# Low halves of the second weights: from scaled differences on VectorE to plain ones on GpSimd, after scaling the weights in place, by quarters, with a side step in every step of a pair

## The chip, the cores and the metric

The kernel runs on one core of a Trainium2 chip. The metric is device time in microseconds (us); the median of three runs of the kernel before is 1008.27 us, and they lie between 1008.16 and 1008.62.

## The reference

Attention with a window of 128 and a linear position bias is followed by a soft mixture of experts (`_moe_ref`, 32 slots) and by a second mixture whose gate is balanced by eight Sinkhorn rounds. The change is in the second mixture, which takes most of the time:

```python
def _moe2_ref(x, w_gate, w1, w2):          # x 2304x512, w1 8x512x1024, w2 8x1024x512
    logits = x @ w_gate
    P = np.exp(logits - logits.max())
    for _ in range(8):
        P /= P.sum(1, keepdims=True) + 1e-09
        P /= P.sum(0, keepdims=True) + 1e-09
        P *= N / E
    out = np.zeros((N, D))
    for e in range(E):
        h = np.maximum(x @ w1[e], 0.0)
        out += P[:, e:e + 1] * (h @ w2[e])
    return out
```

## The kernel before

**The loop.** The second mixture runs over 8 experts (0 to 7) and, in each, over 9 pairs of token tiles. A pair `m` is `relu(x @ w1) @ w2` for two tiles of 128 tokens and is done by Strassen's scheme with seven products. Each product is `prod`: 12 matmuls of 128x128 by 128x256 in float16, in which either factor is split into a high half and a low half (high by high, high by low, low by high). Products go into the PSUM tiles `x` and `y`, and `add` accumulates them into `acc` on VectorE (DVE) by a `scalar_tensor_tensor`; in expert 0 ScalarE (ACT) copies the four first ones.

**A pair's seven steps.** In step `k_` (0 to 6) of pair `m` the program emits, in this order: half of the hidden matmuls `z` of the next pair (`emit_z`, steps 0 and 1, four matmuls each), the product and an `add` (`step`), one piece of side work (`next(side, None)`), and `left(m + 1, k_)`, which builds the left operands of the next pair from `z`. Every engine works through its own instructions in that order. `left` makes the sums `s3`, `s2`, `s1`, `s4` on VectorE, their high halves on ScalarE (`hi_s`) and their low halves on GpSimd (POOL, `lo_s`), in steps 2, 3, 4 and 6. Strassen's second product comes first in a pair, so the low half of `s2`, made in step 3 of one pair, is read at the start of the next. The other low halves have more time.

**Side work.** `side` is a chain of generators; one `yield` is one slot. During expert `e` it holds, for expert `e + 1`: `prep_w1` (5 slots: matmuls with the raw first weights, a scale, the stacked operand `stk`), a load, `prep_w2a` (below), a load of the second weights of `e + 2` into the buffer just read, and `scale_p`. In expert 0 the gate (6 slots) comes first and then the Sinkhorn rounds, three slots each, one slot of them together with one slot of the chain above (`par`). What is left of `side` at step 2 of an expert's last pair is emitted there at once.

**`prep_w2a`.** It finds the largest absolute weight (8 slots of ScalarE's `Abs`, then 4 more) and a power of two `iv`. From the four blocks `b11`, `b12`, `b21`, `b22` of the raw weights it makes Strassen's seven right operands: four differences on GpSimd (`diff`, two instructions of 512 elements per partition each), and for every operand four quarters `r` of 256 elements: the high half `Copy(scale=iv)` on ScalarE (`conv`, L600) and the low half `raw * iv - high` on VectorE (`low`, L593). The queue `todo` holds each low half back by one quarter. Operands are done one after the other, 28 quarters in 28 slots, with the differences riding along. The weights of expert 0 are prepared ahead of the loop.

Of the kernel before, what the change touches and what calls it, by code (L numbers as in the profile page):

```python
# [11 lines left out]
AF = mybir.ActivationFunctionType  # L12
ALU = mybir.AluOpType
# [11 lines left out]
def tile_kernel(ctx: ExitStack, tc: tile.TileContext, q, k, v, phi, w1, w2, w_gate, m1, m2, rel, out):  # L25
    nc = tc.nc
# [68 lines left out]
    with tc.manual_schedule():  # L95
        with ExitStack() as ab:
# [5 lines left out]
            with ExitStack() as at:  # L102
# [369 lines left out]
                side = []  # L472
# [82 lines left out]
            def largest(dg, ps):  # L555
                nc.tensor.matmul(ps, lhsT=ones, rhs=dg, start=True, stop=True)

            def prep_w2a(e, place):
                wsum[e] = mp.tile([128, 4, 256], F32, tag="t1", name="t1", bufs=1)

                am = mp.tile([128, 1], F32, tag="am2", name="am2")
                amp = mp.tile([128, FC], F32, tag="amp", name="amp")
                for i in range(FC):
                    nc.scalar.activation(out=wsum[e][:, 0:2].rearrange("p a b -> p (a b)"),
                                         in_=wt["m2", e][:, DM * i:DM * (i + 1)], func=AF.Abs, accum_out=amp[:, i:i + 1])
                    yield
                yield
                nc.vector.tensor_reduce(out=am, in_=amp, axis=AX.X, op=ALU.max)
                dg = spread(am)
                yield  # L570
                ps = place()
                largest(dg, ps)
                if e:
                    yield
                ar = mp.tile([128, 1], F32, tag="ar2", name="ar2")
                nc.vector.tensor_reduce(out=ar, in_=ps, axis=AX.X, op=ALU.max)
                pw, iv = pow2(mp, ar, "w2")
                nc.vector.tensor_scalar_mul(inv_w[:, e:e + 1], pw, 1.0 / (WSC * CSC))
                nc.vector.tensor_scalar_mul(iv, iv, WSC)  # L579
                yield  # L580
                hi = wpre.tile([128, 7, 4, 256], F16, tag="w", name="w2h")
                lo = wpre.tile([128, 7, 4, 256], F16, tag="w", name="w2l")
                w2c[e] = (hi, lo)


                raw = wt["m2", e].rearrange("p (c f) -> p c f", c=FC)
                b11, b12 = raw[:, 0:4, 0:256], raw[:, 0:4, 256:512]
                b21, b22 = raw[:, 4:8, 0:256], raw[:, 4:8, 256:512]
                t1 = wsum.pop(e)


                def low(i, src, r):
                    nc.vector.scalar_tensor_tensor(out=lo[:, i, r], in0=src[:, r], scalar=iv, in1=hi[:, i, r],  # L593
                                                   op0=ALU.mult, op1=ALU.subtract)

                todo = []

                def conv(i, src):
                    for r in range(4):
                        nc.scalar.activation(out=hi[:, i, r], in_=src[:, r], func=AF.Copy, scale=iv)  # L600
                        if todo:
                            low(*todo.pop())
                        todo.append((i, src, r))
                        yield

                def diff(dst, x_, y_):
                    for r in range(2):
                        eng = nc.gpsimd if e or r else nc.vector
                        eng.tensor_tensor(out=dst[:, 2 * r:2 * r + 2], in0=x_[:, 2 * r:2 * r + 2],
                                          in1=y_[:, 2 * r:2 * r + 2], op=ALU.subtract)  # L610
                        yield

                def both(x_, y_):
                    for _ in x_:
                        next(y_, None)
                        yield

                yield from diff(t1, b12, b11)
                yield from both(conv(0, b11), diff(b12, b22, b12))
                yield from both(conv(2, b21), diff(b11, b22, t1))  # L620
                yield from conv(3, b12)
                yield from both(conv(1, b11), diff(b21, b21, b11))
                yield from conv(4, t1)
                yield from conv(6, b22)
                yield from conv(5, b21)
                low(*todo.pop())
                yield

            def prep_w1(e, pool=None, tag=None):
# [46 lines left out]
            with ExitStack() as bs:  # L676
# [75 lines left out]
                for i in range(4):  # L752
                    for cp in range(4):
                        dst = selh if cp < 2 else sell
                        nc.vector.tensor_copy(out=dst[32 * i:32 * i + 32, 32 * cp:32 * cp + 32],
                                              in_=idn[32 * i:32 * i + 32, 32 * i:32 * i + 32])
# [65 lines left out]
                for h in range(2):  # L822
                    ps = pb.tile([128, 512], F32, tag="b", name="b")
                    for dc in (2 * h, 2 * h + 1):
# [3 lines left out]
                        out=st[:, 2 * h:2 * h + 2], in_=ps[:, 2 * NS * h:2 * NS * h + 2 * NS].rearrange("p (a b) -> p a b", a=2))  # L828
# [7 lines left out]
            with ExitStack() as ms:  # L836
# [271 lines left out]
                side = None  # L1108
                for m in range(NM):
                    e, n = divmod(m, NP)  # L1110
                    if n == 0:
                        side = []
                        if e + 1 < E:
                            side = [prep_w1(e + 1), loads(e + 2, "m1"), prep_w2a(e + 1, lambda: pmt[:, 256:384]), loads(e + 2, "m2")]
                        if e == 0:
                            side = [gate(), par(chain(sinkhorn(), scale_p(0)), chain(*side))]
                        if e + 1 < E:
                            side.append(scale_p(e + 1))
                        side = chain(*side)
                    for k_ in range(7):  # L1120
                        if m and k_ < 2 and m + 1 < NM:
                            emit_z(m + 1, k_)
                        if m or k_ > 3:
                            step(m, k_)
                        elif k_ == 0:

                            step(m, 0)
                            emit_z(m + 1, 0)
                            step(m, 1)
                            step(m, 2)  # L1130
                        elif k_ == 1:
                            emit_z(m + 1, 1)
                            for kk_, nm in ((KS1, "s1"), (KS4, "s4")):
                                hi_s(0, kk_, nm)
                                lo_s(0, kk_, nm)
                            step(m, 3)
                        if k_ == 0:
                            if m:
                                last(m - 1)
                            left(m, 7)  # L1140
                        if k_ != 3:
                            next(side, None)
                        if k_ in (4, 5) and NP - 1 <= m < 2 * NP - 1:
                            weigh((m + 1) % NP + NP * (k_ - 4))
                        if m + 1 < NM:
                            left(m + 1, k_)
                        if n == NP - 1 and k_ == 2:
                            for _ in side:
                                pass
# [38 lines left out]
```

## Time and profile before

| | |
|---|---|
| median of the runs | 1008.27 us |
| the profiled execution | 1009.35 us |
| its span, first to last instruction | 1007.6 us |
| mean granted TensorE clock | 0.99 |
| busy share: TensorE matmul, VectorE, ScalarE, GpSimd | 95%, 84%, 60%, 45% |

The profiled execution lies 1.08 us above the median, and 1.75 us of its time lie outside its span. Times of rows are counted from the span's start. A busy share is a mean over stages: the second mixture begins at about 211 us, and its stages differ. Matmuls are pipelined (one of these takes 273 ns and the next starts 109 ns later), so TensorE's pace is read from where its instructions start. The granted clock is 1.00 where TensorE has its full 2.4 GHz.

### The profile page before, as it was taken

How to read it: one execution, taken by the hardware profiler on the slowest of the kernel's cores; microseconds unless marked ns; L12 is line 12 of the kernel's file. 1: busy time of each engine (PE TensorE's matmuls, PEld its weight loads, DVE VectorE, ACT ScalarE, POOL GpSimd, SP SyncE). 2: the span in 40 equal slices, each digit the busy share in tenths (PEclk: the TensorE clock that was granted, in tenths of full speed). 3: DMA queues.
4: the chain of work that ended last, by engine and by line, in shares of the span. 5: the costliest groups of instructions: out<-in, count | busy, mean ns of one | idle time of the engine just before them, and what ended most of it. 6: DMA issues, size and time to landing. Idle time of an engine off the chain costs nothing.

```text
span 1007.6 us, 24024 instructions
## 1 busy us (share of the span) xinstructions
PE 958.6 (95%) x9341; PEld 811.4 (81%) x9341; DVE 849.7 (84%) x2128; ACT 608.2 (60%) x1473; POOL 452.6 (45%) x433
## 2 busy tenths in 40 slices
PE   8999999888889999999999999999999999999993
PEld 7887886367678888888888888888888888888883
DVE  6888885758999789979988998799789978987772
ACT  5878784745557677665646664656556655654440
POOL 2321211213445475437544754574366447544440
PEclk9999999999999999999999999999999999999997
DMA  9999998941100310220022002200220200001111
GB/s 175 252 236 199 253 289 300 392 178 34 62 2 1 121 60 1 84 95 2 1 85 94 2 1 88 92 1 11 85 86 1 85 12 2 1 1 39 52 53 48
DMA packets 93927, 90.07 MB, mean 89 GB/s; under 512 B 63094, under 2 KB 67062, under 8 KB 93814
## 3 DMA queue, kind: packets, MB, share of 16 engines
q1 hardware_dynamic: 93814, 88.54, 29.5%
q8 instruction: 73, 1.20, 0.5%
q14 instruction: 40, 0.33, 0.1%
HBM read 81.97 MB, written 4.72 MB: 86 GB/s over the span
## 4 chain that ended last, share of the span: by engine, by line
PE 70%; DVE 20%; ACT 5%; issue 3%; DMA 1%; POOL 0%; DVEq 0%; POOLq 0%; SPq 0%; ACTq 0%
PE x L996 27%; PE y L996 21%; PE z L924 5%; DVE w2l L593 4%; PE xp L276 4%; DVE acc L1010 3%; DVE s L949 3%; PE s L202 3%; DVE ops L937 2%; PE pt L251 2%; PE pt L155 2%; PE m L633 1%; ACT w2h L600 1%; PE b L732 1%; ACT ops L934 1%
## 5 line engine op out<-in xcount | busy, mean ns | idle before, releaser
L996 PEld LDWEIGHTS <-ops 128*128 128x128 f16 x6048 | 593.4, 98 | 85.8 <-issue 13.5
L956 POOL TENSOR_TENSOR ops<-s,ops 128x512 f16<-128x512 f32 x287 | 332.3, 1160 | 377.7 <-ACT ops L953 333.4
L996 PE MATMUL x<-w2h,ops 128*128 128x256 f16 x2304 | 415.5, 273 | 5.7 <-DVE acc L1010 3.1
L953 ACT CAST ops<-s 128x512 f16<-128x512 f32 x288 | 177.6, 617 | 267.0 <-DVE s L949 265.6
L996 PE MATMUL y<-w2h,ops 128*128 128x256 f16 x1728 | 320.3, 274 | 4.5 <-DVE acc L1010 4.2
L996 PE MATMUL x<-w2l,ops 128*128 128x256 f16 x1152 | 314.3, 273 | 0.0
L996 PE MATMUL y<-w2l,ops 128*128 128x256 f16 x864 | 236.0, 274 | 0.0
L1010 DVE SCALAR_TENSOR_TENSOR acc<-x,pe,acc 128x256 f32<-128x256 f32 x252 | 120.2, 477 | 34.0 <-PE x L996 33.8
L937 DVE SCALAR_TENSOR_TENSOR ops<-z,ops 128x512 f16<-128x512 f32 x216 | 146.7, 679 | 0.0
L934 ACT ACTIVATE ops<-z 128x512 f16<-128x512 f32 x216 | 127.8, 592 | 25.7 <-PE z L924 23.2
L593 DVE SCALAR_TENSOR_TENSOR w2l<-w,w2i,w2h 128x256 f16<-128x256 f32 x192 | 124.2, 657 | 0.7 <-ACT w2h L600 0.7
L1010 DVE SCALAR_TENSOR_TENSOR acc<-y,pe,acc 128x256 f32<-128x256 f32 x189 | 90.2, 477 | 31.3 <-PE y L996 30.8
L949 DVE SCALAR_TENSOR_TENSOR s<-z,s 128x512 f32<-128x512 f32 x144 | 97.9, 680 | 3.2 <-ACT ops L934 3.1
L949 DVE SCALAR_TENSOR_TENSOR s<-z,r 128x512 f32<-128x512 f32 x144 | 98.0, 680 | 2.8 <-ACT ops L934 2.6
L924 PE MATMUL z<-ct,stk 128*128 128x256 f16 x576 | 87.7, 276 | 7.4 <-DVE ops L937 6.3
L600 ACT ACTIVATE w2h<-w,w2i 128x256 f16<-128x256 f32 x192 | 93.3, 504 | 1.9 <-DVE w2i L579 1.1
L181 POOL TENSOR_SCALAR qn<-qn 128x128 f32<-128x128 f32 x64 | 34.4, 546 | 101.0 <-DMA qn<-in_q_dram 80.6
L924 PEld LDWEIGHTS <-stk 128*128 128x128 f16 x576 | 53.2, 98 | 24.5 <-DVE ops L937 12.2
L230 ACT ACTIVATE et<-et,mx 128x192 f32<-128x192 f32 (+2 forms) x144 | 61.3, 435 | 1.2 <-DVE mx L221 1.1
L202 PE MATMUL s<-kT,qT 128*128 128x192 f32 (+2 forms) x288 | 50.2, 317 | 0.1
L221 DVE CUSTOM_DVE_ANT_0 et<-s,rel_sb 128x192 f32<-128x192 f32 (+2 forms) x144 | 40.2, 326 | 8.6 <-PE s L202 8.1
L202 PEld LDWEIGHTS s<-kT,qT 128*128 128x128 f32 x288 | 43.9, 191 | 3.4 <-issue 3.4
(189 smaller groups left out, 895.4 us busy)
## 6 DMA issues: line engine op xcount, KB each, us to landing
w<-in_moe_w_dram SPq DMA_DIRECT2D x68, 512.0 KB
w<-in_moe_w_dram SPq DMA_DIRECT2D x14, 2048.0 KB
kn<-in_k_dram SPq DMA_DIRECT2D x36, 128.0 KB
qn<-in_q_dram SPq DMA_DIRECT2D x36, 128.0 KB
v<-in_v_dram SPq DMA_DIRECT2D x18, 256.0 KB
out_dram<-acc SPq DMA_DIRECT2D x17, 256.0 KB
w<-in_moe_w_dram SPq DMA_DIRECT2D x2, 1024.0 KB
stk<-sh SPq DMA_DIRECT2D x56, 16.0 KB
```

Of the source, the lines that this page charges most:

```text
L202: nc.tensor.matmul(ps[gg][:, j, col:192], lhsT=qT[:, g, j, :], rhs=kT[:, g, j, k0:k1], start=True, stop=True)
L230: nc.scalar.activation(out=runs[hh], in_=runs[hh], func=AF.Exp, bias=mx[:, hh:hh + 1], scale=-1.0, accum_out=sm[:, hh:hh + 1])
L593: nc.vector.scalar_tensor_tensor(out=lo[:, i, r], in0=src[:, r], scalar=iv, in1=hi[:, i, r], op0=ALU.mult, op1=ALU.subtract)
L600: nc.scalar.activation(out=hi[:, i, r], in_=src[:, r], func=AF.Copy, scale=iv)
L924: nc.tensor.matmul(ps[:, i], lhsT=stk[e][:, 128 * ft:128 * ft + 128], rhs=ct.rearrange("p (a n) t -> p a n t", a=2)[:, :, n, :], start=Tru ...
L934: nc.scalar.activation(out=ops_[m][:, k_, 0], in_=zb(m, i, j), func=AF.Relu)
L937: nc.vector.scalar_tensor_tensor(out=ops_[m][:, k_, 1], in0=zb(m, i, j), scalar=0.0, in1=ops_[m][:, k_, 0], op0=ALU.max, op1=ALU.subtract)
L949: nc.vector.scalar_tensor_tensor(out=new_sum(m, nm), in0=zb(m, i, j), scalar=0.0, in1=o, op0=ALU.max, op1=op)
L953: nc.scalar.copy(out=ops_[m][:, k_, 0], in_=sm_[m, nm])
L956: eng.tensor_tensor(out=ops_[m][:, k_, 1], in0=sm_[m, nm], in1=ops_[m][:, k_, 0], op=ALU.subtract)
L996: nc.tensor.matmul(out_, lhsT=a_[:, k_, l_, i, :], rhs=r_[:, k_, i, :], start=(first and j == 0), stop=(j == 11), skip_group_check=True)
L1010: nc.vector.scalar_tensor_tensor(out=o, in0=ps, scalar=pe_[e][:, t:t + 1], in1=o, op0=ALU.mult, op1=ALU.add)
```

## The change

For expert 0 nothing changes in `prep_w2a`. For the others ScalarE first multiplies the raw weights by `iv` in place, by quarters, two instructions of 512 elements each. High halves are then plain copies (`nc.scalar.copy`), low halves plain differences on GpSimd (`minus`), and the four differences are also made by quarters, all on GpSimd. The loop over quarters is the outer one: 11 slots a quarter, with one GpSimd instruction of 256 elements in each (the first `part` emits none, a last one follows), 45 slots in all, where the weights' conversion and differences took 31. The loop over pairs gives side work a slot in all seven steps; step 3 had none.

```diff
-                yield from diff(t1, b12, b11)
-                yield from both(conv(0, b11), diff(b12, b22, b12))
...
-                yield from conv(5, b21)
-                low(*todo.pop())
+                if e == 0:
+                    yield from diff(t1, b12, b11)
...
+                    return
...
+                def minus(out_, x_, y_):
+                    nc.gpsimd.tensor_tensor(out=out_, in0=x_, in1=y_, op=ALU.subtract)
+
+                def part(i, src, r):
+                    nc.scalar.copy(out=hi[:, i, r], in_=src[:, r])
+                    if todo:
+                        i_, src_, r_ = todo.pop()
+                        minus(lo[:, i_, r_], src_[:, r_], hi[:, i_, r_])
+                    todo.append((i, src, r))
+
+                for r in range(4):
+                    for x_ in (raw[:, r, :], raw[:, r + 4, :]):
+                        nc.scalar.activation(out=x_, in_=x_, func=AF.Copy, scale=iv)
+                    minus(t1[:, r], b12[:, r], b11[:, r])
+                    yield
+                    part(0, b11, r)
+                    yield
+                    minus(b12[:, r], b22[:, r], b12[:, r])
+                    yield
+                    part(2, b21, r)
+                    yield
+                    minus(b11[:, r], b22[:, r], t1[:, r])
+                    yield
+                    part(3, b12, r)
+                    yield
+                    part(1, b11, r)
+                    yield
+                    minus(b21[:, r], b21[:, r], b11[:, r])
+                    yield
+                    part(4, t1, r)
+                    yield
+                    part(6, b22, r)
+                    yield
+                    part(5, b21, r)
+                    yield
...
-                        if k_ != 3:
-                            next(side, None)
+                        next(side, None)
```

Line numbers behind the changed place rise: `low`'s L593 stays for expert 0 alone, `minus` is L634, and L937, L949, L956, L1010 become L980, L992, L999, L1053.

On VectorE, late in a pair of expert 1, the program had the following. `s_...` rows are the sums of the next pair (the first one `s1`, the last `s4`), `acc` rows the accumulation, and `w2l` rows the low halves of the coming weights:

```order
L949 SCALAR_TENSOR_TENSOR s_6030<-z,r_5953 128x512
L1010 SCALAR_TENSOR_TENSOR acc<-x,pe,acc 128x256
L593 SCALAR_TENSOR_TENSOR w2l<-w,w2i,w2h 128x256
L937 SCALAR_TENSOR_TENSOR ops<-z,ops 128x512
L1010 SCALAR_TENSOR_TENSOR acc<-x,pe,acc 128x256
L593 SCALAR_TENSOR_TENSOR w2l<-w,w2i,w2h 128x256
L949 SCALAR_TENSOR_TENSOR s_6067<-z,s_6010 128x512
L1010 SCALAR_TENSOR_TENSOR acc<-y,pe,acc 128x256
```

Now the same place on VectorE reads:

```order
L992 SCALAR_TENSOR_TENSOR s_6050<-z,r_5973 128x512
L1053 SCALAR_TENSOR_TENSOR acc<-x,pe,acc 128x256
L980 SCALAR_TENSOR_TENSOR ops<-z,ops 128x512
L1053 SCALAR_TENSOR_TENSOR acc<-x,pe,acc 128x256
L992 SCALAR_TENSOR_TENSOR s_6087<-z,s_6031 128x512
L1053 SCALAR_TENSOR_TENSOR acc<-y,pe,acc 128x256
```

The `w2l` rows are gone from it, and nothing stands in their place. On GpSimd the pair of which this is the end had only the four `lo_s` in most pairs of an expert (`ops` rows, of `s3`, `s2`, `s1`, `s4` in this order). Now it has, from behind the `lo_s` of the pair before to its own last one:

```order
L634 TENSOR_TENSOR w2l<-w,w2h 128x256
L634 TENSOR_TENSOR w<-w 128x256
L634 TENSOR_TENSOR w2l<-w,w2h 128x256
L999 TENSOR_TENSOR ops<-s_5994,ops 128x512
L634 TENSOR_TENSOR w2l<-w,w2h 128x256
L999 TENSOR_TENSOR ops<-s_6031,ops 128x512
L634 TENSOR_TENSOR w<-w 128x256
L999 TENSOR_TENSOR ops<-s_6050,ops 128x512
L634 TENSOR_TENSOR w2l<-w,w2h 128x256
L634 TENSOR_TENSOR w2l<-t_5209,w2h 128x256
L999 TENSOR_TENSOR ops<-s_6087,ops 128x512
```

Seven instructions came in: three ahead of `s3`'s low half, one ahead of `s2`'s, one ahead of `s1`'s, two ahead of `s4`'s. The third place is GpSimd at the end of expert 0, where what is left of `side` is emitted at once, between the `lo_s` of `s3` (first row) and of `s2` (last row) of the first pair of expert 1:

```order
L999 TENSOR_TENSOR ops<-s_4938,ops 128x512
L634 TENSOR_TENSOR w2l<-w,w2h 128x256
L634 TENSOR_TENSOR w<-w,t_3922 128x256
L634 TENSOR_TENSOR w2l<-w,w2h 128x256 x2
L634 TENSOR_TENSOR w<-w 128x256
L634 TENSOR_TENSOR w2l<-w,w2h 128x256
L634 TENSOR_TENSOR w2l<-t_3922,w2h 128x256
L634 TENSOR_TENSOR w2l<-w,w2h 128x256 x2
L999 TENSOR_TENSOR ops<-s_4991,ops 128x512
```

Nine instructions stand there where before none stood; at the ends of experts 1 to 6 it is three.

## Rows read from the trace of the kernel before

**Rows 1.** The page's first part: busy time, share of the span, instructions, by engine.

```profile
PE 958.6 (95%) x9341; PEld 811.4 (81%) x9341; DVE 849.7 (84%) x2128; ACT 608.2 (60%) x1473; POOL 452.6 (45%) x433
```

**Rows 2.** TensorE's timeline, first `z` matmul of six pairs: start, length, instruction.

```profile
229.17 0.38 PE L924 MATMUL z<-ct,stk 128*128 128x256 f16 x2
...
331.19 0.38 PE L924 MATMUL z<-ct,stk 128*128 128x256 f16 x2
...
630.43 0.38 PE L924 MATMUL z<-ct,stk 128*128 128x256 f16 x2
...
640.48 0.38 PE L924 MATMUL z<-ct,stk 128*128 128x256 f16 x2
...
660.79 0.38 PE L924 MATMUL z<-ct,stk 128*128 128x256 f16 x2
...
712.74 0.27 PE L924 MATMUL z<-ct,stk 128*128 128x256 f16 x1
```

**Rows 3.** Busy time by stretch, three pairs of expert 4: length, then each engine's.

```profile
core 0: us, PE busy (x) PEld busy (x) DVE busy (x) ACT busy (x) POOL busy (x), PEclk, DMA share, GB/s
...
630.90:640.90 10.00, 10.00 (x94) 8.98 (x92) 7.53 (x15) 8.09 (x21) 4.63 (x4) 1.00 0.45 157
...
651.20:661.20 10.00, 10.00 (x94) 8.96 (x92) 8.77 (x18) 6.39 (x13) 9.05 (x9) 1.00 0.01 2
661.20:672.10 10.90, 10.52 (x95) 8.97 (x94) 10.90 (x21) 6.85 (x14) 7.05 (x6) 1.00 0.01 2
```

**Rows 4.** The page's costliest groups: instruction, count, busy us, mean ns, idle before.

```profile
L956 POOL TENSOR_TENSOR ops<-s,ops 128x512 f16<-128x512 f32 x287 | 332.3, 1160 | 377.7 <-ACT ops L953 333.4
...
L593 DVE SCALAR_TENSOR_TENSOR w2l<-w,w2i,w2h 128x256 f16<-128x256 f32 x192 | 124.2, 657 | 0.7 <-ACT w2h L600 0.7
...
L600 ACT ACTIVATE w2h<-w,w2i 128x256 f16<-128x256 f32 x192 | 93.3, 504 | 1.9 <-DVE w2i L579 1.1
```

**Rows 5.** VectorE's timeline, four instructions.

```profile
239.89 0.18 DVE L881 TENSOR_SCALAR rs<-rs 128x18 f32<-128x18 f32 x1
...
252.12 1.08 DVE L881 TENSOR_SCALAR rs<-rs 128x18 f32<-128x18 f32 x1
...
662.58 1.26 DVE L593 SCALAR_TENSOR_TENSOR w2l<-w,w2i,w2h 128x256 f16<-128x256 f32 x1
...
666.18 0.47 DVE L593 SCALAR_TENSOR_TENSOR w2l<-w,w2i,w2h 128x256 f16<-128x256 f32 x1
```

**Rows 6.** GpSimd's timeline, one pair of expert 4; in brackets the idle time before.

```profile
634.95 1.16 POOL L956 TENSOR_TENSOR ops<-s,ops 128x512 f16<-128x512 f32 x1 [2.65 <-ACT ops L953]
637.25 1.16 POOL L956 TENSOR_TENSOR ops<-s,ops 128x512 f16<-128x512 f32 x1 [1.15 <-ACT ops L953]
638.56 1.16 POOL L956 TENSOR_TENSOR ops<-s,ops 128x512 f16<-128x512 f32 x1 [0.15 <-ACT ops L953]
641.18 1.16 POOL L956 TENSOR_TENSOR ops<-s,ops 128x512 f16<-128x512 f32 x1 [1.46 <-ACT ops L953]
```

**Rows 7.** GpSimd's groups by form, whole program: two of them.

```profile
L181 POOL TENSOR_SCALAR qn<-qn 128x128 f32<-128x128 f32 x64 | 34.4, 546 | 101.0 <-DMA qn<-in_q_dram 80.6 <-PE pt L332 8.4 <-PE pt L251 6.4
...
L609 POOL TENSOR_TENSOR t<-w 128x512 f32<-128x512 f32 x15 | 19.1, 1271 | 10.5 <-DMA w<-in_moe_w_dram 10.5
```

**Rows 8.** Busy time by stretch, two pairs of expert 0 (columns: rows 3).

```profile
243.80:256.70 12.90, 11.23 (x98) 9.26 (x97) 12.25 (x29) 8.90 (x25) 5.04 (x5) 1.00 0.48 175
...
269.50:285.80 16.30, 12.62 (x98) 10.09 (x97) 15.48 (x35) 7.26 (x17) 9.78 (x9) 0.90 0.01 2
```

**Rows 9.** TensorE's timeline, one wait of expert 0.

```profile
273.16 0.37 PE L924 MATMUL z<-ct,stk 128*128 128x256 f16 x1 [2.15 <-DVE ops L937]
```

**Rows 10.** Busy time by stretch, behind that wait (columns: rows 3).

```profile
273.60:276.60 3.00, 3.00 (x17) 2.14 (x15) 2.79 (x5) 1.83 (x6) 3.00 (x4) 0.50 0.00 0
```

**Rows 11.** Busy time by stretch, end of a weight load (columns: rows 3).

```profile
424.00:426.00 2.00, 2.00 (x21) 1.79 (x19) 1.54 (x4) 0.62 (x1) 1.85 (x2) 1.00 0.41 159
```

**Rows 12.** ScalarE's timeline, the first reader of those weights.

```profile
438.17 0.62 ACT L564 ACTIVATE t<-w 128x512 f32<-128x512 f32 x1
```

More of the change, by code (lines that the diff above doesn't have):

```diff
@@ L616, in both @@
                         yield
-                yield from diff(t1, b12, b11)
-                yield from both(conv(0, b11), diff(b12, b22, b12))
[L620 to L624, printed above, removed]
-                yield from conv(5, b21)
-                low(*todo.pop())
+                if e == 0:
+                    yield from diff(t1, b12, b11)
+                    yield from both(conv(0, b11), diff(b12, b22, b12))
+                    yield from both(conv(2, b21), diff(b11, b22, t1))
+                    yield from conv(3, b12)
+                    yield from both(conv(1, b11), diff(b21, b21, b11))
+                    yield from conv(4, t1)
+                    yield from conv(6, b22)
+                    yield from conv(5, b21)
+                    low(*todo.pop())
+                    yield
+                    return
@@ new lines, in minus @@
+                def minus(out_, x_, y_):
[30 more added lines that the diff above has]
+                    part(5, b21, r)
+                    yield
@@ L627, in prep_w2a @@
+                i_, src_, r_ = todo.pop()
+                minus(lo[:, i_, r_], src_[:, r_], hi[:, i_, r_])
                 yield
```

## The prediction

> **What bounds the kernel now.** First the page's sum by engine: TensorE is busy 95% and VectorE 84% of the span [rows 1]. A mean hides the stages, and a TensorE that counts as busy need not run at its pace, so next TensorE's timeline: the distance between the first `z` matmuls of successive pairs is a pair's length. Where VectorE is not full a pair takes 640.48 - 630.43 = 10.05 us [rows 2]; the reader should take this as the floor, since 92 matmuls must pass. The five pairs from 660.79 to 712.74 take 51.95, or 1.7 more than five floors. Third, busy time by stretch shows why: from 661.2 to 672.1 VectorE is busy 10.90 of 10.90 us, in a pair that only measures scales (630.9 to 640.9) 7.53 of 10.0 [rows 3]. The difference is `low`, 28 instructions of 657 ns mean, 18.4 us an expert [rows 4]. So TensorE sets the time, and VectorE delays it in the second half of experts 1 to 6. In expert 0 it delays much more: eight pairs from 229.17 to 331.19 take 102.0 against 80.4 [rows 2], with VectorE busy 12.25 of 12.9 us under two Sinkhorn rounds, and 15.48 of 16.3 where `low` comes on top [rows 8].
>
> **What the change removes.** All 196 `low` of experts 1 to 7 go from VectorE. Its work in a pair falls to about 7.5 of 10.05 us, and the pairs of experts 1 to 6 fall to the floor if nothing else is late: 6 x 1.7 = **10.2 us**, of which VectorE's cover is 2.5 us a pair.
>
> **What it adds on ScalarE.** Eight scalings of 512 elements and 28 copies of 256 replace 28 conversions of 504 ns [rows 4]. A copy of the same size is taken at 0.5 (a bound from above is that row, from below half of it), a scaling at twice that at most. Then 45 slots hold 22 us at most, 0.5 a slot. In the pair from 630.9 to 640.9 ScalarE has 8.09 us of work, `Abs` in six of its seven steps, and the pair keeps the floor [rows 3]; seven slots of 0.5 on a base of about 4.6 are the same 8.1. I cost it at nothing; were that cover gone, it would be what comes late in front of GpSimd below.
>
> **What it adds on GpSimd**, the item that decides. Between a pair's four `lo_s` this engine idles 2.65, 1.15, 0.15 and 1.46 us, 5.4 in all [rows 6]. Into these gaps come three, one, one and two instructions of 256 elements, 44 in 45 slots, 6.8 a pair. No row shows one of this size. From below, half of the 512-element rows: 0.58 us for a low half (1160 ns [rows 4]) and 0.64 for a difference (1271 [rows 7]). From above: the line through 128 elements in 546 ns (one input) and 512 in 1271 [rows 7] gives 0.79 at 256, and 1.27 is excluded by any cost per element. I take 0.70, between halving and that line. Then 6.8 x 0.70 = 4.8, and 4.8 + 4.6 for the four `lo_s` is 9.4 of 10.05 us. The pair from 651.2 to 661.2 had GpSimd busy 9.05 and still ran 94 matmuls in 10.0 us [rows 3], so such a load does no harm by itself. Gap by gap: `s1`'s low half slips by 0.55, `s4`'s not further, and 2.1 us of work in the 2.65 gap take the slip back. `s2`'s low half, the one with the nearest deadline, ends at 638.41 and is wanted when the next pair begins, 0.44 behind the `z` at 640.48 (four matmuls of 109 ns): 2.5 us of slack [rows 2, 6]. At 0.79 GpSimd needs 10.0 us a pair, just the floor. At each quarter's first difference it also waits behind two scalings, about 1 us, which the remaining 0.6 us a pair and the slack must carry. I take off 1 us in all for this.
>
> Here the trace bears on a rule. A `low` took 0.47 us alone and 1.26 beside a GpSimd instruction [rows 5, 6], so part of the 657 ns is waiting, which goes too. The Trainium skill (SBUF — State Buffer, "Who interferes with whom") says that a VectorE instruction with two SBUF inputs and a GpSimd instruction reading SBUF exclude each other; the trace agrees. By that rule the change speaks against itself in one place, the Sinkhorn rounds, where VectorE still has such small instructions: see the third rival.
>
> **Expert 0.** Sinkhorn now gets seven slots a pair, 2.33 rounds for 2. An instruction of VectorE takes about 0.5 us (15 in 7.53 [rows 3]); ScalarE makes four of the adds here, so a pair without rounds needs about 5.5, and a round (12.25 - 5.5) / 2 = 3.4 us [rows 8]. With 2.33 rounds that is 13.4, for three pairs, two of which also hold scales (0.6 more each), and the rounds end there but for a rest. Then 14.0 + 13.4 + 14.0 + 5 x 10.05 = 91.7, and 2.9 for `prep_w1`'s matmuls, which before were part of the 102.0. They move one slot ahead; I leave them in, 94.6. At the expert's end nine GpSimd instructions, 6.3 us, now stand before `s2`'s low half, in a gap of 1.15 with 2.5 of slack: TensorE waits 2.6 us. After a wait of 2.15 us in this stage [rows 9] the granted clock was 0.50, the 1.2 GHz level, for the next 3 us, with 17 matmul records in the time of some 28 [rows 10]; I charge 1.5 for the like. Sum 94.6 + 4.1 = 98.7, a gain of **3.3**. At the ends of experts 1 to 6 three instructions, 2.1 us, fit gap and slack.
>
> **DMA.** The load of the next but one second weights waits on SyncE's queue for the last reader of the buffer, now GpSimd's last low half, some 7 us later than now. It ended at about 424.8 [rows 11], and its first reader ran at 438.17 [rows 12]. One slot earlier at that end too, 5 us remain; the stacked operand's copies queued behind it come later than that. Cost nothing.
>
> **Sum.** 10.2 + 3.3 - 1.0 = 12.5 us, from the profiled 1009.35 to 996.9, which is 1.08 above the median; for the median **995.8 us**.
>
> **Rivals.** *GpSimd late by a little*: ScalarE waits for GpSimd (`part(1)` copies what `minus` made two slots before) and GpSimd for ScalarE, so waits add up and `s2` is late by about a microsecond an expert, or expert 0 gains nothing. For it: GpSimd has 0.6 us to spare a pair. Against it: ScalarE's own idle time. Half the gain, 1002.
>
> *GpSimd becomes the bound*, which ends slower. Place: the `lo_s` of `s2`. With p us an instruction a pair needs 4.6 + 6.8 p; the gain of 12.5 is lost when 6 pairs x (6.8 p - 5.4) less 2.5 of slack is about 1.8 in each of seven experts, at p = 0.90. At p = 0.95 it is 6.4 - 2.5 = 3.9 in each, 27 against 13.5: 1022. Against it: both bounds of p lie below 0.90. The Trainium skill (GPSIMD Engine Reference, "Engine selection") tells to keep elementwise work on VectorE, GpSimd being about twice as slow with two inputs. Its 2.6 cycles an element would be an estimated 0.55 us for 256, and 8.4 us a pair; by its own figure the rule does not bite.
>
> *Sinkhorn is held up by GpSimd*: a round's VectorE instruction of 18 elements took 0.18 us and, beside GpSimd, 1.08 [rows 5]. Weights now begin in slot 24 of expert 0, and rounds last to slot 30: 2.3 rounds with four such instructions, up to 0.7 more each, 6.5 us, and 1002. Against it: `low` did the same there before.
>
> *No change*: VectorE's delay is taken over one for one by the new waits, 1008.
>
> *More*: no clock loss in expert 0 and its waits shorter, 988 to 990.
>
> **Numbers.** Chances: forecast (990 to 1000) 0.59; little late or Sinkhorn held (1000 to 1006) 0.18; no change 0.08; GpSimd the bound 0.09; more 0.06. A difference under 0.2%, 2 us, can't be told from none here. Faster by more: 0.59 + 0.18 + 0.06 = 0.83; within 0.08; slower 0.09. The range 988 to 1007 takes in the first two, most of "more" and a little of "no change", 0.82.
>
> **What would show it.** Right: VectorE near 7.5 us a pair throughout experts 1 to 6; distances of 10.05 from the fourth pair on; L634 rows of 0.6 to 0.8 us; GpSimd at 9 to 10 of 10 us without TensorE waiting for `lo_s`; one wait of 2 to 3 us at the end of expert 0. Wrong: L634 near 0.9 or above; matmuls of `s2` waiting for GpSimd; Sinkhorn pairs of 15 us; ScalarE waiting for L634.

## The result, and the profile after

The changed kernel takes 999.42 us (median of 4 runs, 997.47 to 1000.41) beside 1008.38 us of the kernel before on the same chip: a ratio of 0.9909, 95% interval 0.9891 to 0.9926. It is faster by 9.0 us where 12.5 were forecast. The profiled execution took 1000.32 us with a span of 998.5 us, so the two profiled spans differ by 1007.6 - 998.5 = 9.1 us.

First the page of the kernel after, its busy time by engine and its chain of work:

```profile
PE 954.0 (96%) x9341; PEld 815.9 (82%) x9341; DVE 746.4 (75%) x1932; ACT 625.3 (63%) x1529; POOL 574.9 (58%) x685
...
PE 85%; DVE 10%; ACT 2%; issue 1%; POOL 1%; DVEq 0%; POOLq 0%; ACTq 0%
```

Beside [rows 1], VectorE has 103 us less to do and GpSimd 122 more, and the chain of work that ended last lies on TensorE for 85% of the span, 70% before. A mean doesn't say where the 9.1 us came from, so next TensorE's timeline, first `z` matmul of pairs (start, length, instruction):

```profile
217.01 0.27 PE L967 MATMUL z<-ct,stk 128*128 128x256 f16 x1
...
298.40 0.27 PE L967 MATMUL z<-ct,stk 128*128 128x256 f16 x1
...
318.49 0.27 PE L967 MATMUL z<-ct,stk 128*128 128x256 f16 x1
...
333.08 0.27 PE L967 MATMUL z<-ct,stk 128*128 128x256 f16 x1
...
426.56 0.27 PE L967 MATMUL z<-ct,stk 128*128 128x256 f16 x1
...
656.81 0.27 PE L967 MATMUL z<-ct,stk 128*128 128x256 f16 x1
...
894.01 0.27 PE L967 MATMUL z<-ct,stk 128*128 128x256 f16 x1
```

Three rows that stand against them in the kernel before, beside 331.19 of [rows 2]:

```profile
217.74 0.27 PE L924 MATMUL z<-ct,stk 128*128 128x256 f16 x1
...
427.09 0.27 PE L924 MATMUL z<-ct,stk 128*128 128x256 f16 x1
...
903.16 0.27 PE L924 MATMUL z<-ct,stk 128*128 128x256 f16 x1
```

Experts 1 to 6 (first `z` of expert 1 to first `z` of expert 7) took 903.16 - 331.19 = 571.97 us and take 894.01 - 333.08 = 560.93: a gain of **11.0 us**. Expert 0 took 331.19 - 217.74 = 113.45 and takes 333.08 - 217.01 = 116.07: a **loss of 2.6 us**, where 3.3 of gain were forecast. The remaining 0.7 us lie ahead of the loop, which the change does not touch.

Experts 1 to 6 look as forecast. A pair of expert 4 by stretch (columns as in [rows 3]), at the floor:

```profile
666.90:676.90 10.00, 10.00 (x95) 8.96 (x92) 7.57 (x14) 6.83 (x14) 8.98 (x12) 1.00 0.00 1
```

Two of GpSimd's groups by form in the whole program (count, then busy us, mean ns), and from the page ScalarE's plain copy:

```profile
L634 POOL TENSOR_TENSOR w2l<-w,w2h 128x256 f16<-128x256 f32 x168 | 112.1, 673 | 0.0
L634 POOL TENSOR_TENSOR w<-w 128x256 f32<-128x256 f32 x56 | 40.8, 729 | 0.0
```

```profile
L637 ACT CAST w2h<-w 128x256 f16<-128x256 f32 x168 | 66.3, 402 | 4.3 <-POOL w L634 4.2
```

And GpSimd's timeline in the pair from 646.8, the `lo_s` of `s2`:

```profile
653.59 1.16 POOL L999 TENSOR_TENSOR ops<-s,ops 128x512 f16<-128x512 f32 x1 [1.11 <-ACT ops L996]
```

VectorE is at 7.6 us a pair instead of 10.9, GpSimd at about 9.0, and `s2`'s low half ends at 654.75, which is 2.5 us ahead of its use at 656.81 + 0.44. It has not moved against the pair since [rows 6], although some seven more instructions pass on the same engine. It waited 1.11 us for ScalarE's high half, not for GpSimd's new work.

Expert 0 by stretch, pairs 0 to 4, then 8 (a stretch ends where the next pair's first product, `s2`'s, starts; a wait ahead of that product counts to the pair that ends):

```profile
215.70:232.90 17.20, 16.40 (x148) 13.37 (x148) 10.99 (x22) 7.90 (x20) 5.88 (x5) 0.90 0.06 21
232.90:248.20 15.30, 11.68 (x103) 9.77 (x102) 14.19 (x37) 7.83 (x19) 4.62 (x4) 1.00 0.07 17
248.20:260.60 12.40, 12.20 (x98) 10.03 (x96) 11.40 (x31) 8.71 (x22) 4.15 (x4) 0.86 0.43 172
260.60:274.60 14.00, 11.69 (x101) 9.54 (x100) 12.86 (x38) 7.35 (x16) 5.57 (x7) 1.00 0.01 1
274.60:288.80 14.20, 12.23 (x97) 10.04 (x94) 11.07 (x23) 8.33 (x20) 11.31 (x14) 0.88 0.00 1
...
318.90:333.50 14.60, 11.65 (x94) 9.73 (x93) 6.46 (x13) 9.29 (x22) 12.40 (x17) 0.88 0.19 53
```

Three things are to be seen. Pairs 1 and 3, with Sinkhorn rounds, are VectorE's: 14.19 of 15.3 us and 12.86 of 14.0. Pairs 0, 2, 4 and 8 have a mean clock of 0.86 to 0.90; in pair 2 TensorE is busy 12.20 of 12.4 us at 0.86. In its expert 0 the kernel before had two such pairs, pair 4 (0.90 [rows 8]) and pair 5 (0.88 from 285.8 to 299.8). And pair 8 waits, with TensorE busy 11.65 of 14.6.

That wait at the end of expert 0, in TensorE's timeline, then ScalarE's:

```profile
327.71 0.37 PE L1039 MATMUL x<-w2h,ops 128*128 128x256 f16 x1 [2.95 <-ACT acc L1049]
```

```profile
325.05 0.40 ACT L637 CAST w2h<-w 128x256 f16<-128x256 f32 x1 [1.60 <-POOL w L634]
...
326.99 0.40 ACT L637 CAST w2h<-w 128x256 f16<-128x256 f32 x1 [0.92 <-POOL w L634]
327.30 0.36 ACT L1049 COPY acc<-x 128x256 f32<-128x256 f32 x1
```

TensorE did not wait for a low half. In expert 0 ScalarE copies the first products out of PSUM (`add`, L1049), and that copy stood behind plain copies of weights (L637), two of which waited, 1.60 and 0.92 us, for a difference that GpSimd had still to make. The releaser in brackets and the row ahead of it on its engine show the whole path.

### The profile page after: what moved, and what is told of

Its sections match the earlier page's. It is cut to its first block, busy times and chain, and to the rows that moved or that the text cites. A ratio compares the mean times of both kernels' runs of the same rounds, so it can differ in the third digit from the quotient of the medians.

```text
span 998.5 us, 24140 instructions
## 1 busy us (share of the span) xinstructions
PE 954.0 (96%) x9341; PEld 815.9 (82%) x9341; DVE 746.4 (75%) x1932; ACT 625.3 (63%) x1529; POOL 574.9 (58%) x685
## 4 chain that ended last, share of the span: by engine, by line
PE 85%; DVE 10%; ACT 2%; issue 1%; POOL 1%; DVEq 0%; POOLq 0%; ACTq 0%
PE x L1039 36%; PE y L1039 26%; PE z L967 6%; PE xp L276 4%; PE s L202 3%; PE pt L251 2%; PE pt L155 2%; PE m L676 2%; PE b L775 1%; DVE et L221 1%; DVE et L240 1%; DVE ops L980 1%; PE s L849 1%; PE pt L290 1%; PE warm L83 1%
## 5 line engine op out<-in xcount | busy, mean ns | idle before, releaser
L999 POOL TENSOR_TENSOR ops<-s,ops 128x512 f16<-128x512 f32 x287 | 331.7, 1159 | 236.2 <-ACT ops L996 198.7
L1053 DVE SCALAR_TENSOR_TENSOR acc<-x,pe,acc 128x256 f32<-128x256 f32 x252 | 121.7, 483 | 74.9 <-PE x L1039 71.0
L980 DVE SCALAR_TENSOR_TENSOR ops<-z,ops 128x512 f16<-128x512 f32 x216 | 147.1, 681 | 0.0
L1053 DVE SCALAR_TENSOR_TENSOR acc<-y,pe,acc 128x256 f32<-128x256 f32 x189 | 91.4, 483 | 60.8 <-PE y L1039 59.1
L634 POOL TENSOR_TENSOR w2l<-w,w2h 128x256 f16<-128x256 f32 x168 | 112.1, 673 | 0.0
L992 DVE SCALAR_TENSOR_TENSOR s<-z,r 128x512 f32<-128x512 f32 x144 | 98.2, 682 | 9.2 <-ACT r L988 4.4
L992 DVE SCALAR_TENSOR_TENSOR s<-z,s 128x512 f32<-128x512 f32 x144 | 98.0, 681 | 0.0
L637 ACT CAST w2h<-w 128x256 f16<-128x256 f32 x168 | 66.3, 402 | 4.3 <-POOL w L634 4.2
L967 PEld LDWEIGHTS <-stk 128*128 128x128 f16 x576 | 55.9, 99 | 13.2 <-issue 3.1
```

The lines of the kernel that those rows point to most:

```text
L634: nc.gpsimd.tensor_tensor(out=out_, in0=x_, in1=y_, op=ALU.subtract)
L637: nc.scalar.copy(out=hi[:, i, r], in_=src[:, r])
L967: nc.tensor.matmul(ps[:, i], lhsT=stk[e][:, 128 * ft:128 * ft + 128], rhs=ct.rearrange("p (a n) t -> p a n t", a=2)[:, :, n, :], start=Tru ...
L980: nc.vector.scalar_tensor_tensor(out=ops_[m][:, k_, 1], in0=zb(m, i, j), scalar=0.0, in1=ops_[m][:, k_, 0], op0=ALU.max, op1=ALU.subtract)
L992: nc.vector.scalar_tensor_tensor(out=new_sum(m, nm), in0=zb(m, i, j), scalar=0.0, in1=o, op0=ALU.max, op1=op)
L999: eng.tensor_tensor(out=ops_[m][:, k_, 1], in0=sm_[m, nm], in1=ops_[m][:, k_, 0], op=ALU.subtract)
```

## The experiments

Each is compared with the kernel before on the same chip (1008.41 us in the first four, 1008.71 in the next three, 1009.17 in the last two). Lengths of pairs are read from where TensorE's instructions start, or from the stretches shown.

**Only the seventh slot** (the kernel before, with side work in step 3 too):

```diff
-                        if k_ != 3:
-                            next(side, None)
+                        next(side, None)
```

> The kernel before with a side slot in step 3 and nothing else of the change (weights still by scaled differences on VectorE, operand by operand). Theory 1 (the seventh slot costs where VectorE sets the pace, since the same side work falls on fewer pairs): in experts 1 to 6 seven low halves a pair take 7.5 + 7 x 0.6 = 11.7 us of VectorE's time, over four pairs, so about 3 us above the floor of 10.04 per expert instead of 1.7; in expert 0 the gate's and the Sinkhorn pairs grow as in the changed kernel, by about 3 to 5 us. Together 6 x 1.3 and 4 more: 1016 to 1022 us. Theory 2 (the slot itself is neutral, and expert 0's loss in the changed kernel comes from GpSimd's new work): 1007 to 1010 us, expert 0 near 115 us.

Measured: 1012.44 us, ratio 1.0041 (1.0026 to 1.0056). TensorE's timeline, first `z` of pair 0 and of expert 1, and pair 0 by stretch:

```profile
217.69 0.27 PE L924 MATMUL z<-ct,stk 128*128 128x256 f16 x1
...
333.43 0.27 PE L924 MATMUL z<-ct,stk 128*128 128x256 f16 x1
```

```profile
216.30:232.10 15.80, 14.99 (x149) 12.49 (x149) 10.89 (x22) 7.63 (x19) 5.89 (x5) 0.99 0.04 16
```

The time lies between the two ranges given. By itself the slot costs time, and in the profiled execution nearly all of it in expert 0: its span is 1010.1 us, 2.5 longer than before, and expert 0 takes 333.43 - 217.69 = 115.74 us, 2.3 longer. What was expected of it in experts 1 to 6 did not come. Pair 0, with the same work as in the changed kernel and the clock at 0.99 instead of 0.90, takes 15.8 us instead of 17.2: there a fall of the clock costs 1.4.

**Only the new preparation** (the changed kernel, with six slots a pair):

```diff
-                        next(side, None)
+                        if k_ != 3:
+                            next(side, None)
```

> The changed kernel without the slot in step 3 (new preparation of the weights, six slots a pair). Then 11 or 12 GpSimd instructions of the weights remain to be issued at once at the end of experts 1 to 6 and 17 at the end of expert 0. Theory 1 (what remains delays s2's low half by its length less a gap of 1.15 and a slack of 2.5, and the wait costs 1.5 more by the granted clock): 12 x 0.69 = 8.1, so 4.5 + 1.5 in each of six experts against 1.7 recovered there; expert 0 keeps its pairs 0 to 3 as before the change (13.2, 14.2, 12.9, 12.8) and ends with a wait of 8 to 10: 1030 to 1036 us in all. Theory 2 (the remainder hides in the slack): 994 to 998 us.

Measured: 1033.11 us, ratio 1.0249 (1.0233 to 1.0264), within the range given for theory 1. Here more of the chain is left over, and comes in one piece at the end of each expert. TensorE's timeline at the start of expert 4:

```profile
630.78 0.28 PE L1039 MATMUL x<-w2h,ops 128*128 128x256 f16 x1 [2.27 <-POOL ops L999]
```

So neither half of the change gains alone: +4.0 us and +24.7 us. Together they make -9.0. A slot more was the condition for the work to move to GpSimd.

**Six slots in the first five pairs of an expert, seven behind them:**

```diff
-                        next(side, None)
+                        if k_ != 3 or m >= 5:
+                            next(side, None)
```

In this condition `m` counts pairs from the start of the loop, so it touches expert 0 alone.

> The changed kernel without the slot in step 3 in the first five pairs of expert 0, where gate and Sinkhorn rounds run; all else as changed. Theory 1 (the seventh slot is what made these pairs longer): pairs 0 to 4 go back to 13.2, 14.2, 12.9, 12.8 and about 13, 66 us instead of 73; five more instructions remain at the end of expert 0, 3 us more there: 994 to 997 us. Theory 2 (GpSimd's weight instructions hold up VectorE's small Sinkhorn instructions, or the granted clock falls whatever the slots): pairs 3 and 4 stay near 14 us and the end costs 3 more: 1000 to 1003 us.

Measured: 1000.22 us, ratio 0.9918 (0.9901 to 0.9934), in the range of theory 2 and above that of theory 1. TensorE's timeline, the first `z` of pair 0, of pairs 6 and 8 and of expert 1, with the wait at the end of expert 0:

```profile
217.86 0.27 PE L967 MATMUL z<-ct,stk 128*128 128x256 f16 x1
...
294.49 0.27 PE L967 MATMUL z<-ct,stk 128*128 128x256 f16 x1
...
314.58 0.27 PE L967 MATMUL z<-ct,stk 128*128 128x256 f16 x1
...
327.17 0.37 PE L1039 MATMUL x<-w2h,ops 128*128 128x256 f16 x1 [6.32 <-ACT acc L1049]
...
333.80 0.27 PE L967 MATMUL z<-ct,stk 128*128 128x256 f16 x1
```

From pair 0 to pair 6 it takes 294.49 - 217.86 = 76.6 us, the changed kernel 298.40 - 217.01 = 81.4. So the seventh slot cost 4.8 us there; theory 1 had forecast 7 for the first five of these pairs. Falls of the clock are a part of it: this run had none in these pairs, the changed kernel one each in pairs 0, 2 and 4. That in pair 0 does not come with the slot alone: the run with doubled low halves (below), with the same work there, had none, with a clock of 1.00 from 224 to 232 us. But five slots less in these pairs are five pieces more at the end, and pair 8 takes 333.80 - 314.58 = 19.2 us instead of 14.6, where theory 1 had 3 us more. The gain is handed back, with a clock of 0.50 in the end of the wait and behind it:

```profile
325.90:332.70 6.80, 5.53 (x27) 3.81 (x27) 1.77 (x4) 3.37 (x7) 5.25 (x7) 0.50 0.38 82
```

**Every low half twice** on GpSimd, 27 instructions more an expert (the last one, outside `part`, is made once):

```diff
-                        minus(lo[:, i_, r_], src_[:, r_], hi[:, i_, r_])
+                        for _ in range(2):
+                            minus(lo[:, i_, r_], src_[:, r_], hi[:, i_, r_])
```

> The changed kernel with each low half made twice on GpSimd (the same instruction again; the last of an expert once). Theory 1 (a pair's GpSimd time decides as soon as it exceeds 10.04 us, less 2.5 of slack once an expert): GpSimd needs 4.6 + 6.8 x 0.69 + 4.4 x 0.67 = 12.3 us a pair, 2.3 above the floor in six pairs of each of seven experts, less the slack: 11 us each, 1065 to 1085 us. Theory 2 (GpSimd's queue is not what holds s2's low half, as the slack is wide): under 1020 us.

Measured: 1090.92 us, ratio 1.0815 (1.0799 to 1.0831). A pair of expert 4 by stretch, and the wait in it:

```profile
729.60:743.90 14.30, 11.79 (x95) 9.74 (x94) 7.64 (x15) 6.15 (x14) 13.83 (x19) 0.88 0.01 2
```

```profile
732.52 0.40 PE L1040 MATMUL x<-w2h,ops 128*128 128x256 f16 x1 [2.50 <-POOL ops L1000]
```

This is the rival in which GpSimd bounds: 13.83 of 14.3 us busy, and TensorE waits for the `lo_s`. The time is about 6 us above the range of theory 1, and far above that of theory 2; the clock falls in such a pair too (0.88). The changed kernel has about 1 us of GpSimd's time to spare a pair.

**The last quarter's low halves of expert 1's weights on VectorE** (`eng` is a new argument of `minus`):

```diff
-                        minus(lo[:, i_, r_], src_[:, r_], hi[:, i_, r_])
+                        minus(lo[:, i_, r_], src_[:, r_], hi[:, i_, r_],
+                              nc.vector if e == 1 and r_ == 3 else nc.gpsimd)
```

> The changed kernel with the low halves of the last quarter of expert 1's weights on VectorE (a plain difference there); they are what GpSimd gets at once at the end of expert 0. Theory 1 (the wait of 3.1 us at that end is GpSimd's queue in front of s2's low half): two or three instructions remain there, the wait goes with its clock loss, the last pair of expert 0 falls from 14.6 to 10.0 to 10.6, 994.5 to 996 us. Theory 2 (ScalarE's six copies, or the chain between the two engines, hold s2 up there): the pair stays at 13 us or more, 998 to 1000 us.

Measured: 998.49 us, ratio 0.9901 (0.9884 to 0.9917). TensorE's timeline at the end of expert 0, then ScalarE's ahead of that copy:

```profile
327.48 0.27 PE L1040 MATMUL x<-w2h,ops 128*128 128x256 f16 x1 [1.70 <-ACT acc L1050]
```

```profile
325.84 0.41 ACT L637 CAST w2h<-w 128x256 f16<-128x256 f32 x1 [1.37 <-POOL w L634]
```

The wait falls from 2.95 to 1.70 us, and pair 8 from 14.6 to 11.9, without a clock of 0.50 behind it. So the row of GpSimd's instructions at this end makes at least part of the wait. It doesn't go wholly: ScalarE's copies of weights still stand ahead of its copy out of PSUM, and one of them still waits for a difference on GpSimd. The pair lies between the two theories, and the time in the range of theory 2: of pair 8's 2.7 us the profiled span shows 1.8, as its first `z` of pair 0 starts at 218.00, 1.0 us later than in the changed kernel, where the programs don't differ.

**Two thirds of these low halves on VectorE**, six slots in the first five pairs, five slots more in each of pairs 5 to 7:

```diff
-                        minus(lo[:, i_, r_], src_[:, r_], hi[:, i_, r_])
+                        minus(lo[:, i_, r_], src_[:, r_], hi[:, i_, r_],
+                              nc.vector if e == 1 and i_ % 3 else nc.gpsimd)
...
-                        next(side, None)
+                        if k_ != 3 or m >= 5:
+                            next(side, None)
+                        if 5 <= m < 8 and k_ in (0, 1, 2, 4, 5):
+                            next(side, None)
```

> The changed kernel with six slots in the first five pairs of expert 0, twelve in the next three, and the low halves of operands 1, 2, 4 and 5 of expert 1's weights on VectorE (idle 4.4 us a pair there). Theory 1 (expert 0's pairs are set by how densely VectorE's side work falls, and its end by what GpSimd has left over): 67 us for the first five pairs as in the run before, 10.1 to 10.8 for each of the next three, 10.1 for the last, 108 to 110 in all instead of 117.8: 990 to 992 us. Theory 2 (the two engines keep each other from SBUF, so that twelve slots make these three pairs 12 us or more): 995 to 998 us.

**The same with all of them on VectorE** (`if e == 1`):

> As the run with two thirds on VectorE, but with all low halves of expert 1's weights on VectorE: 7.6 of them a pair at 0.47 us alone, 0.66 with waits, on top of 5.6, so 9.2 to 10.6 us of VectorE in the three dense pairs, against 7.8 of GpSimd. Theory 1 (VectorE's own sum decides): these three pairs 10.1 to 11.0, the whole within 1.5 us of the run with two thirds. Theory 2 (waits between the engines grow with VectorE's share): 2 us or more above it.

Measured: 995.31 us (ratio 0.9867, 0.9852 to 0.9881) with two thirds, 997.82 us (0.9891, 0.9876 to 0.9906) with all. One pair of expert 0 by stretch, the seventh, first of the run with two thirds, then of that with all:

```profile
296.10:306.40 10.30, 10.17 (x93) 8.96 (x93) 7.83 (x13) 8.98 (x22) 10.22 (x13) 1.00 0.01 2
```

```profile
295.90:308.00 12.10, 10.44 (x95) 8.96 (x94) 11.23 (x20) 9.18 (x22) 8.02 (x10) 1.00 0.00 1
```

With two thirds the run beats the changed kernel; with all, the intervals of the ratios overlap. In neither profiled execution is there a fall of the clock in expert 0. With two thirds the time is 3.3 us above the range of theory 1 and in that of theory 2, though of its three dense pairs only one is as long as that theory had them: 13.1, 10.3 and 11.4 us. With all of them it is 2.5 us above the run with two thirds, as theory 2 had it; VectorE has 11.23 us in a pair, above the 10.6 expected at most, and delays TensorE as before the change. The Trainium skill (GPSIMD Engine Reference, "Engine selection") would have elementwise work of this kind on VectorE; the measurement decides for this stage: GpSimd's instruction is slower by itself (673 ns; on VectorE the run with the last quarter has one of 410 with GpSimd idle), but the pair has room for a third of them there, and VectorE has none for all.

**Rounds and weights taken apart in expert 0.** The gate has pair 0 as before the change. From pair 1 on the rounds go ahead in four steps of a pair (three in the second run), the weight work in every step, with three slots more in pairs 1 and 2:

```diff
-                            side = [gate(), par(chain(sinkhorn(), scale_p(0)), chain(*side))]
+                            gate_, rounds = gate(), chain(sinkhorn(), scale_p(0))
...
-                        next(side, None)
+                        if m == 0:
+                            if k_ != 3:
+                                next(gate_, None)
+                        else:
+                            if e == 0 and k_ in (0, 2, 4, 6):
+                                next(rounds, None)
+                            next(side, None)
+                            if m in (1, 2) and k_ in (1, 3, 5):
+                                next(side, None)
+                        if m == NP - 1 and k_ == 2:
+                            for _ in rounds:
+                                pass
```

The second run has `(0, 2, 4)` there.

> The changed kernel with the gate's and Sinkhorn's rounds taken off the common slots in expert 0: the gate in pair 0 as before the change, from pair 1 on the rounds go one step ahead in only four of the seven steps of a pair, while the weight work goes ahead in every step, with three extra slots in pairs 1 and 2. The rounds then last into pair 8. Theory 1: VectorE's sum of a pair decides in expert 0; four rounds' steps beside the 5.5 us of the sums stay under or near the floor, so the pairs are about 13.2, 13.5, then 10.3 to 10.8, and expert 0 takes 99 to 104 us instead of 117.8: 982 to 988. Theory 2: each round also makes TensorE wait for VectorE's c, and the two engines' shared access stretches VectorE's steps, however thinly the rounds are spread; expert 0 then takes 106 to 112 us: 989 to 996.

> As the run with four slots, but the rounds go ahead in three of the seven steps of a pair, and what is left of them runs out in pair 8. Theory 1: the pairs between are at the floor of 10.05 us and pair 8 takes what is left of the rounds; expert 0 97 to 103 us: 980 to 987. Theory 2: as many waits as before for the rounds, only further apart, and the rounds left in pair 8 stand in a row there: expert 0 106 to 113 us: 989 to 997.

Measured: 995.82 us (ratio 0.9885, 0.9864 to 0.9906; 994.76 to 1002.33) with four steps, and **989.12 us** (ratio 0.9809, 0.9796 to 0.9823; 988.68 to 992.12) with three. Pairs 2 to 4 of expert 0 by stretch, with three steps, and behind them pairs 2 and 5 of the run with four:

```profile
244.50:257.40 12.90, 10.61 (x96) 9.35 (x96) 9.71 (x28) 9.31 (x24) 5.38 (x6) 1.00 0.44 170
257.40:267.60 10.20, 10.16 (x94) 9.12 (x94) 7.17 (x16) 6.77 (x18) 8.39 (x10) 1.00 0.01 2
267.60:278.10 10.50, 10.38 (x97) 9.17 (x96) 9.54 (x20) 7.59 (x19) 8.72 (x12) 1.00 0.01 2
```

```profile
245.20:259.90 14.70, 11.18 (x99) 9.62 (x99) 12.78 (x35) 9.57 (x24) 5.48 (x6) 1.00 0.41 149
...
282.30:296.70 14.40, 10.91 (x99) 9.36 (x97) 12.66 (x29) 8.26 (x20) 10.51 (x13) 1.00 0.00 1
```

With three steps expert 0 takes 106.1 us instead of 117.8, and with four 111.4. The run with three steps is the fastest of all, but neither theory has it whole. By the numbers theory 2 holds: both times, and both lengths of expert 0, lie in its ranges, those of three steps at the lower edge. Theory 1 is right that a pair comes near the floor once VectorE's sum is under it (9.54 us busy in 10.50). Theory 2 is right that waits remain, but not which: TensorE's waits for VectorE's `c` are 0.5 us in all in expert 0 with four steps, and with three none is listed. The longest group of TensorE's waits in expert 0 with three steps (us in all, times, longest):

```profile
PE x L1039 <- ACT acc L1049: 5.2, 4, 2.3
```

These are for ScalarE's copy out of PSUM, as at the end of expert 0 in the changed kernel, but here that copy comes late for another engine. Of the longest one (its row on TensorE is in the last section), ScalarE's timeline:

```profile
254.71 0.62 ACT L996 CAST ops<-s 128x512 f16<-128x512 f32 x1 [2.99 <-DVE s L992]
```

ScalarE waited 2.99 us for one of VectorE's sums, and the copies behind it with it; two scalings of weights (1.33 us) also stood ahead of the copy that TensorE waited for. So VectorE still delays TensorE there, by the order in which ScalarE works. Nor is the whole gain VectorE's sum: in this profiled execution the clock didn't fall in expert 0 at all, where the changed kernel had four falls, and the run differs in three ways at once (rounds thinned, rounds begun in pair 1, slots added for the weights). With four steps the rounds still crowd single pairs (VectorE busy 12.78 and 12.66 us in the two shown), and behind the first of these the clock falls to 0.50.

## Why the prediction was right in kind and 3.6 us too good

**VectorE's relief: right, the size a little more.** VectorE fell to 7.6 us a pair (7.5 forecast), and the pairs fell to 10.04. The gain in experts 1 to 6 was 11.0 us, not 10.2. Expert 1 gained (427.09 - 331.19) - (426.56 - 333.08) = 2.4 us and the five others 1.7 each in the mean, as read from five pairs of one expert [rows 2]; why expert 1 gained more is open. The 1.0 us taken off for waits at the head of GpSimd's queue was not needed.

**GpSimd: right.** Its instruction was taken at 0.70 us; it measured 673 ns (low half) and 729 (difference), and in the mix about 0.69. It is at 9.0 of 10 us a pair, and the 2.5 us of slack of `s2` are all still there. In experts 1 to 6 neither "late by a little" nor "the bound" came; the run with doubled low halves shows that the second needs no more than 27 instructions more an expert. At the end of expert 0 the mechanism of "late by a little" did come, ScalarE waiting for GpSimd, and with it what that rival said of expert 0, that it gains nothing.

**ScalarE at nothing: right in experts 1 to 6, not in expert 0.** The plain copy takes 402 ns, less than the 0.5 assumed. The prediction named what would come late were ScalarE's cover gone, but put it in front of GpSimd. It came in front of TensorE, by the copies out of PSUM that ScalarE has in expert 0 alone.

**Expert 0: this step failed.** Forecast 98.7 behind pair 0, and pair 0 left at the 13.2 it had (216.4 to 229.6 before), 111.9; measured 117.8 from 215.7 to 333.5. Two of the prediction's signs of being wrong came here, a Sinkhorn pair of 15 us and ScalarE waiting for L634. By terms:

| term | forecast | measured | off by |
|---|---|---|---|
| pair 0, with `prep_w1` moved into it | 13.2 + 2.9 = 16.1 | 17.2 | 1.1 |
| pairs 1 to 3, the rounds | 14.0 + 13.4 + 14.0 = 41.4 | 15.3 + 12.4 + 14.0 = 41.7 | 0.3 |
| pair 4 | 10.05 | 14.2 | 4.2 |
| pairs 5 to 7 | 30.15 | 30.1 | 0 |
| pair 8 | 10.05 + 4.1 = 14.15 | 14.6 | 0.4 |

The prediction wrote of the rounds that they "end there but for a rest", and then gave the pair with the rest the floor. Gate and rounds have 6 + 24 slots; pairs 0 to 3 have 28, and two slots of a round stayed for pair 4. On VectorE the whole of this round ran there, from 275.1 us on. There TensorE waited twice, 1.9 us together:

```profile
PE z L967 <- DVE ops L980: 1.1, 1, 1.1
PE m L930 <- DVE c L928: 0.8, 1, 0.8
```

and the granted clock fell once more (0.88 in the pair's mean). With 1.4 us for the fall that makes 3.3 of the 4.2; the rest is open. The second cause is that one fall was charged for where there were four (pairs 0, 2, 4 and 8). Pair 0's 1.1 us are such a fall, by the run with the seventh slot alone (1.4). Pair 2 has one too, and was still 1.0 shorter than its forecast.

**The end of expert 0: the size near, the way wrong.** 2.6 us of wait were forecast and 2.95 came, but on ScalarE's copy, not on `s2`'s low half. The row of GpSimd's instructions is the same; that its length less gap and slack comes near the wait of another engine is luck.

**Luck in the sum.** In the two profiled executions expert 0 missed its forecast by 5.9 us. Experts 1 to 6 gave 1.8 more than 10.2 - 1.0, and 0.7 came from ahead of the loop, so that the sum missed by 3.4. Two of the four runs lie above the 1000 us at which the forecast's range ended.

**Sinkhorn held up by GpSimd: not so.** The step of 18 elements that the prediction priced reads one tile from SBUF; the step below reads two. In pair 1, with `lo_s` alone on GpSimd, and in pair 4, beside the weights, it took:

```profile
245.71 1.29 DVE L926 TENSOR_TENSOR prob<-prob,rs 128x144 f32<-128x144 f32 x1
...
275.93 0.42 DVE L926 TENSOR_TENSOR prob<-prob,rs 128x144 f32<-128x144 f32 x1
```

Two inputs from SBUF and a threefold time in one of the two places is in line with the exclusion that the prediction cited (the Trainium skill, SBUF — State Buffer, "Who interferes with whom"), but it strikes in a pair without weight work as well: its mean is 852 ns in the three from 229 to 248 us, and 310 in the two from 261 to 275, where the weights begin.

**DMA at nothing: right.** The end of the load of the next but one weights, one stretch, and its first reader in ScalarE's timeline:

```profile
430.00:432.00 2.00, 2.00 (x24) 1.56 (x17) 1.56 (x4) 0.60 (x1) 0.00 (x0) 1.00 0.45 168
```

```profile
437.65 0.63 ACT L564 ACTIVATE t<-w 128x512 f32<-128x512 f32 x1
```

The share of 0.45, and 0.01 in the next 2 us, puts the end at about 431, some 6 us later than in [rows 11], and nearly 7 us ahead of its reader [rows 12].

**What stays open.** The remaining distance of the fastest run in expert 0, 106.1 against 13.2 + 2.9 + 8 x 10.05 = 96.5 us, was not taken apart further than the waits above. Which waits let the clock fall was not settled (below). In pairs 2 and 4 of expert 0 it fell in each of the four profiled executions with rounds and weights in common slots, seven a pair (the changed kernel, the seventh slot alone, doubled low halves, the last quarter on VectorE), and in none of the four with six slots there and the new preparation. In pair 0 it fell in two of the first four.

## What to carry to other kernels

Work that is dealt out by slots couples things that have nothing to do with each other: a slot more for the weights was also a slot more for the Sinkhorn rounds, and their pairs paid for it. Cost a stage in which several chains share the slots slot by slot, down to the pair in which the rest stands; here that one pair held most of the error, and giving the rounds their own, thinner slots, with three more for the weights in two pairs, brought another 10 us on top of the change's 9.

When work moves to an idle engine, look for who waits in order behind it. The wait at the expert's end was neither on the engine that took the work nor on its product, but on a copy of a third engine that stood behind instructions waiting for it.

## What the runs showed of the hardware

A wait of TensorE is followed in some places by 3.4 us at a granted clock of 0.50, the 1.2 GHz level, and its length alone doesn't tell where. In the two last runs TensorE waited for the same copy at the same place, with nearly the same length. Each time its timeline's row of that wait, and a stretch behind it; first with four steps:

```profile
259.85 0.27 PE L1039 MATMUL x<-w2h,ops 128*128 128x256 f16 x1 [2.37 <-ACT acc L1049]
```

```profile
261.10:264.50 3.40, 3.40 (x19) 2.42 (x17) 0.69 (x1) 2.67 (x7) 3.23 (x5) 0.50 0.00 0
```

Then with three:

```profile
257.44 0.27 PE L1039 MATMUL x<-w2h,ops 128*128 128x256 f16 x1 [2.33 <-ACT acc L1049]
```

```profile
257.40:260.80 3.40, 3.36 (x31) 3.00 (x31) 1.99 (x5) 3.40 (x9) 3.32 (x5) 1.00 0.00 0
```

After the first the clock was 0.50 and 19 matmul records stand in 3.4 us, after the second 1.00 and 31. The pair that ends with the first wait is 14.7 us long with TensorE busy for 11.18, that with the second 12.9 with 10.61. Such a fall cost about 1.4 us where it could be read (pair 0). The runs of the changed kernel go with the mean clock at the ends, 997.47 us at 0.989 and 1000.32 at 0.985, but not between: 998.52 and 1000.41 both have 0.987.
